# Second projection product moved into the projection's own PSUM bank, with longer mask and sum operations

## The chip, the core and the metric

The kernel runs on one core of a Trainium2 chip. The metric is the device time in microseconds (us) of one execution; the kernel before takes 344.99 us (median of three runs, 344.81 to 345.07). A core has a matrix engine (TensorE, PE in the profile, with its weight loads as PEld), a vector engine (VectorE, DVE), a scalar engine (ScalarE, ACT), GpSimd (POOL) and SyncE (SP). Each works through its own instruction list in order and waits for the others by semaphores.

## The reference

Sliding-window attention with a linear position bias feeds a gated feed-forward layer:

```python
# attention: 8 batches x 8 heads, 576 tokens, head width 64, window 128
scores = scale * q @ k.T + bias;  masked to 0 <= row - col < 128
x = softmax(scores) @ v                     # -> 4608 tokens x 512
# feed-forward: 512 -> 1536 -> 512
g = x @ w_gate;  val = x @ w_val
out = (g * sigmoid(g) * val) @ w_out        # float32
```

The kernel cuts the 4608 tokens into 9 blocks (n = 0 to 8) of 512 tokens, and the hidden width 1536 into 12 slices (m = 0 to 11) of 128. Heavy products run in float16 with float32 sums in PSUM.

## The kernel before

For blocks 0 to 5 each slice m takes two "wide" products of four 128x512 matmuls, `pg` (gate) and `pv` (value). ScalarE takes tanh of half the gate, VectorE makes `uu`, and VectorE multiplies it by `pv` into `hT`:

```python
    def gate(n, m, pg, c0=0, c1=512):
        ...
        nc.scalar.activation(tt, pg[:, c0:c1], AF.Tanh, scale=0.5)
        nc.vector.scalar_tensor_tensor(out=uu, in0=tt, scalar=one if (n, m) == PIN else 1.0,
                                       in1=pg[:, c0:c1], op0=ALU.add, op1=ALU.mult)
    def val(n, m, pv, c0=0, c1=512):
        ...
        nc.vector.tensor_mul(hT[n][:, m, c0:c1], acted[(n, m)][1][:, c0:c1], pv[:, c0:c1])
```

The projection by `w_out` of blocks 1 to 8 is done with seven products in place of eight (Strassen's scheme in Winograd's form). It needs sums of quarters of `hT`, made on VectorE in three parts per block, after slices 9, 10 and 11:

```python
    def four_sums(a11, a12, a21, a22, s2, s3, s4):
        return [lambda: nc.vector.tensor_sub(s3, a11, a21),
                lambda: nc.vector.tensor_add(a21, a21, a22),
                lambda: nc.vector.tensor_sub(s2, a21, a11),
                lambda: nc.vector.tensor_sub(s4, a12, s2)]

    def sums(n, c):
        ...
        lo, hi = slice(2 * c, 2 * c + 2), slice(HM + 2 * c, HM + 2 * c + 2)
        ...
```

One call of `strassen(n, t)` makes two row groups of 128 tokens; there are two calls (t = 0, 1) for a block. Each `product` is six matmuls of 256 columns. X and Y are the two halves of one PSUM tile `po`, which is a whole bank and of which there is one. `half_plus` is a VectorE operation that empties a half of the bank into an output tile and adds an earlier product:

```python
            po = ps_f.tile([P, 2, HC], FP32, name="po", tag="po", bufs=1)
            X, Y = po[:, 0, :], po[:, 1, :]
            p2 = (ps_f.tile([P, HC], FP32, name="p2", tag="gv") if seeded
                  else ps_a.tile([P, HC], FP32, name="p2", tag="a"))
        ...
        product(X, A11, B11, True)                 # P1
        ... nc.scalar.mul(p1s, X, factor)
        yield
        product(p2, A12, B21, not seeded)          # the second product
        ... half_plus(top[:, 0:HC], p2, p1s)
        yield
        product(X, S2, T2);  nc.scalar.mul(u2s, X, factor)
        yield
        product(Y, S1, T1, end);  nc.scalar.mul(p5s, Y, factor)
        yield
        product(X, S3, T3);  half_plus(low[:, HC:DM], X, p5s)
        yield
        product(Y, S4, B22);  half_plus(top[:, HC:DM], Y, u2s)
        store(n, t, top, ...)
        yield
        product(X, A22, T4);  nc.scalar.mul(low[:, 0:HC], X, factor)
        store(n, t + 2, low, ...)
        yield
```

`seeded` holds for blocks 5 to 7 and `end` for block 8. For blocks 1 to 4 neither holds, and the second product takes one of four banks of the pool `ps_a`, tag "a", which attention uses for its scores (`ps`, `psc`), its weighted values (`av`) and its transposes (`px`, `pt`).

The seven products of a call are woven between the 24 wide products of the next block (their index is 2m for the gate and 2m + 1 for the value); the set AT says after which:

```python
    AT = {1, 3, 4, 6, 8, 9, 11, 12, 14, 16, 17, 19, 20, 22}
            ...
            for m in range(NMB):
                for half, _ in enumerate(gate_val(n, m)):
                    yield 1.0
                    if n > 1 and 2 * m + half in AT:
                        next(parts)
                    ... one or two of the waiting sums are issued here
                ...
                if n > 0 and m >= 9:
                    (at_once if n == 1 and m < 11 else later.extend)(sums(n, m - 9))
```

Attention for later blocks is woven in by a counter. A unit of attention has a tile of exponentials `ex` of eight heads by 256: ScalarE makes it in four parts from four banks of scores, VectorE multiplies it by the mask `reg` in two halves:

```python
        def mul(q4):
            if early_tile:
                return
            o = slice(4 * q4, 4 * q4 + 4)
            nc.vector.tensor_mul(e[:, o, :], e[:, o, :], reg[:, o, :])
        return [[products], [lambda: act(0, 0)], [lambda: act(0, 1), lambda: mul(0)],
                [lambda: act(1, 0)], [lambda: act(1, 1), lambda: mul(1)]]
```

From the start of block 2 the order of the PE list is as the program gives it; the lists of VectorE and ScalarE are ordered by the compiler's scheduler.

Of the kernel before, what the change touches and what calls it, by code (L numbers as in the profile page):

```python
# [10 lines left out]
FP32 = mybir.dt.float32  # L11
# [5 lines left out]
P = 128  # L17
# [19 lines left out]
LATE = 13  # L37
# [14 lines left out]
def kernel(  # L52
# [10 lines left out]
    nc = tc.nc  # L63
    B, H, S, D = q.shape
    NTOK, DM = out.shape
# [79 lines left out]
    ps_f = ctx.enter_context(tc.tile_pool(name="ps_f", bufs=3, space=PSUM))  # L145
    ps_a = ctx.enter_context(tc.tile_pool(name="ps_a", bufs=4, space=PSUM))
# [96 lines left out]
    def scores(i):  # L243

        s, p = units[i]
        def combined(n):
            return scores_128(s, (3, 7, 8)[n], 8, (s, "c", n), msk[n])

        def together(one, two):
            return [one[0] + two[0]] + one[1:] + two[1:]  # L250

        if p == 8:
            first = combined(0) if s == 0 else []
            return first + together(combined(1), combined(2))
        if p == 7 and s == 0:
            return scores_128(s, p, p, (s, p), reg[:, :, 0:P])
        if p == 7:
            return together(scores_128(s, p, p, (s, p), reg[:, :, 0:P]), combined(0))
        if p == 3:
            return scores_128(s, p, p, (s, p), reg[:, :, 0:P], i < FIRST)  # L260
        ks = (9 * s + p) % NK
        banks = []
        early_tile = i < FIRST
        e = epool.tile([P, H, 256], FP16, name="ex", tag="ex", bufs=4)
        ex[(s, p)] = e

        def products():
            for q4 in range(2):
                two = [ps_a.tile([P, 2, 256], FP32, name="ps", tag="a") for _ in range(2)]
                banks.append(two)  # L270
                for par in range(2 if early_tile else 0):
                    o = 4 * q4 + 2 * par
                    nc.tensor.matmul(two[par], idm, bias[:, o:o + 2, :], start=True, stop=False)
                for j in range(2):
                    pair = 2 * q4 + j
                    for par in range(2):
                        rows = slice(64 * par, 64 * par + 64)
                        nc.tensor.matmul(two[par][:, j, :], kT[rows, ks, pair, :],  # L278
                                         qT[rows, p:p + 2, pair, :], start=(j == 0 and not early_tile),
                                         stop=(j == 1))  # L280

        def act(q4, par):
            o = 4 * q4 + 2 * par
            nc.scalar.activation(e[:, o:o + 2, :], banks[q4][par], AF.Exp, scale=scale)  # L284

        def mul(q4):
            if early_tile:
                return
            o = slice(4 * q4, 4 * q4 + 4)
            nc.vector.tensor_mul(e[:, o, :], e[:, o, :], reg[:, o, :])  # L290

        return [[products], [lambda: act(0, 0)], [lambda: act(0, 1), lambda: mul(0)],
                [lambda: act(1, 0)], [lambda: act(1, 1), lambda: mul(1)]]

# [196 lines left out]
        for f in fs:  # L491
            f()

    def sums(n, c):

        if n not in hsum:
            hsum[n] = [spool.tile([P, HM, 256], FP16, name=f"S{i}", tag=f"S{i}") for i in (2, 3, 4)]
        lo, hi = slice(2 * c, 2 * c + 2), slice(HM + 2 * c, HM + 2 * c + 2)
        a11, a12 = hT[n][:, lo, 0:256], hT[n][:, hi, 0:256]
        a21, a22 = hT[n][:, lo, 256:512], hT[n][:, hi, 256:512]  # L500
        s2, s3, s4 = (t_[:, lo, :] for t_ in hsum[n])
        return four_sums(a11, a12, a21, a22, s2, s3, s4)

    def strassen(n, t):

        h = hT[n]
        A11, A12 = h[:, 0:HM, 0:256], h[:, HM:NMB, 0:256]
        S1, A22 = h[:, 0:HM, 256:512], h[:, HM:NMB, 256:512]
        S2, S3, S4 = hsum[n]
        cols = slice(t * P, (t + 1) * P)  # L510
        end = n == NBLK - 1
        seeded = SEVEN_FROM <= n + 1 < NBLK
        factor = 1.0 if n >= SEVEN_FROM else 0.5
        if end:
            X, Y = (ps_a.tile([P, HC], FP32, name="po", tag="a", bufs=4) for _ in range(2))
            p2 = ps_f.tile([P, HC], FP32, name="p2", tag="gv")
        else:
            po = ps_f.tile([P, 2, HC], FP32, name="po", tag="po", bufs=1)
            X, Y = po[:, 0, :], po[:, 1, :]
            p2 = (ps_f.tile([P, HC], FP32, name="p2", tag="gv") if seeded  # L520
                  else ps_a.tile([P, HC], FP32, name="p2", tag="a"))
        top, low = (opool.tile([P, DM], FP32, name="osb", tag="osb") for _ in range(2))
        if end and t:
            spare = [opool.tile([P, DM], FP32, name="osb", tag="osb") for _ in range(2)]
            p1s, p5s, u2s = spare[0][:, 0:HC], spare[0][:, HC:DM], spare[1][:, 0:HC]
        else:
            p1s, p5s, u2s = (supool.tile([P, HC], FP32, name=i, tag=i, bufs=1)
                             for i in ("p1s", "p5s", "u2s"))

        def product(dst, a, b, start=False):  # L530
            for m in range(HM):
                nc.tensor.matmul(dst, a[:, m, cols], b[:, m, :], start=(start and m == 0),  # L532
                                 stop=(m == HM - 1), skip_group_check=True)

        def half_plus(dst, a, b):
            nc.vector.scalar_tensor_tensor(out=dst, in0=a, scalar=factor, in1=b,
                                           op0=ALU.mult, op1=ALU.add)

        product(X, A11, B11, True)
        if seeded:  # L540
            nc.scalar.copy(p2, X)
        else:
            nc.scalar.mul(p1s, X, factor)
        yield
        product(p2, A12, B21, not seeded)
        if seeded:
            nc.vector.tensor_scalar_mul(top[:, 0:HC], p2, factor)
        else:
            half_plus(top[:, 0:HC], p2, p1s)
        if end and t:  # L550
            store(n, t, top, 0, HC)
        yield
        product(X, S2, T2)
        nc.scalar.mul(u2s, X, factor)
        yield
        product(Y, S1, T1, end)
        if end and t:
            nc.vector.tensor_scalar_mul(p5s, Y, factor)
        else:
            nc.scalar.mul(p5s, Y, factor)  # L560
        yield
        product(X, S3, T3)
        half_plus(low[:, HC:DM], X, p5s)
        if end and t:
            store(n, t + 2, low, HC, DM, True)
        yield
        product(Y, S4, B22)
        half_plus(top[:, HC:DM], Y, u2s)
        store(n, t, top, HC if end and t else 0, DM, end)
        yield  # L570
        product(X, A22, T4)
        if end:
            nc.vector.tensor_scalar_mul(low[:, 0:HC], X, factor)
        else:
            nc.scalar.mul(low[:, 0:HC], X, factor)
        store(n, t + 2, low, 0, HC if end and t else DM, end)
        yield
# [31 lines left out]
    later = []  # L609
# [86 lines left out]
                    of[which[0]][name](which[1])  # L696
                yield n, 7 * u + k, name, which

    AT = {1, 3, 4, 6, 8, 9, 11, 12, 14, 16, 17, 19, 20, 22}

    def ffn():

        for n in range(NBLK):
# [8 lines left out]
# [5 lines that stand above are left out]
                        yield 0.75  # L717
                    if n > 1:
                        for _ in range(1 + (len(later) > 3)):
                            if later:  # L720
                                later.pop(0)()
                if n == 1:
                    if m in (4, 6, 8, 10):
                        for _ in project(0, m // 2 - 2, ps_f, "po", 1):
                            yield 1.0
                    if m in (4, 6, 8):
                        weight_sums(m // 2 - 2)
                if n > 0 and m >= 9:
                    (at_once if n == 1 and m < 11 else later.extend)(sums(n, m - 9))
                if n + 1 == SEVEN_FROM:  # L730
                    if m == SILU_AT:
                        attention_ends()
                        by_silu.update((n, i) for i in range(m + 1, NMB))
                    if m in (SILU_AT + 1, SILU_AT + 2):
                        later.extend(gate_val_weight_sums(m - SILU_AT - 1))
                    if m == SILU_AT:
                        later.extend(x_sums(n + 1))
# [267 lines left out]
```

## Time and profile before

| what | value |
|---|---|
| time, median of three runs | 344.99 us |
| span of the profiled execution | 343.0 us |
| PE busy | 329.1 us (96%) |
| VectorE busy | 277.5 us (81%) |
| ScalarE busy | 207.6 us (61%) |
| products of the projection for blocks 1 to 4 | from 97 to 248 us of the span |
| granted PE clock, mean of the span | 0.999 |

The page gives the busy time of each engine over the span and in 40 equal slices (a slice is 8.6 us; a digit is the busy share in tenths). Matmuls are pipelined, and the end of each is modelled, so the busy share of the PE is not its share of useful work: starts of neighbouring matmuls must be compared. A line of the timeline gives start, length, engine, line of the program, operation, what is written from what, how many were merged and, in brackets, the idle time before it and what ended it.

### The profile page before, as it was taken

Reading aid. Unit: us, or ns where it says so; the run is one execution under the profiler, and the core shown is the slowest. Engines: PE = TensorE matmul, PEld = TensorE weight load, DVE = VectorE, ACT = ScalarE, POOL = GpSimd, SP = SyncE. Lnnn points to the kernel's source line nnn. Section 1 sums busy time; section 2 is a strip of 40 time slices with the busy share of each in tenths; the row PEclk is TensorE's granted clock in tenths of the full one; section 3 lists DMA queues with packets and bytes.
Section 4 is the critical chain, followed back from the end, with each engine's and each line's share of the span. In section 5 each row is a group of like instructions: output and inputs, shape, how many; then the busy total and the mean of one; then the engine's idle time right before and its main releaser. Section 6 shows DMA issues by size and latency. Waiting matters only on the chain.

```text
span 343.0 us, 7778 instructions
## 1 busy us (share of the span) xinstructions
PE 329.1 (96%) x2983; PEld 218.2 (64%) x2983; DVE 277.5 (81%) x652; ACT 207.6 (61%) x412; POOL 109.6 (32%) x136
## 2 busy tenths in 40 slices
PE   6999989999999999999999999999999999999995
PEld 3484455444456565656565655565788878888884
DVE  6578886999798679988899999999855975775683
ACT  3758676565666755756556547563467666776640
POOL 8968672649674274844017000000000000000000
PEclk9999999999999999999999999999999999999999
DMA  9999999999999999999979912021101101011024
GB/s 153 169 180 176 161 173 149 83 135 163 131 172 140 158 169 169 122 166 136 157 201 135 160 32 78 15 71 39 63 2 61 63 0 64 8 56 63 0 71 116
DMA packets 160037, 37.37 MB, mean 109 GB/s; under 512 B 147328, under 2 KB 155648, under 8 KB 160000
## 3 DMA queue, kind: packets, MB, share of 16 engines
q0 software_dynamic: 118336, 18.62, 84.1%
q1 hardware_dynamic: 40976, 17.64, 28.3%
q10 hardware_dynamic: 688, 0.62, 0.6%
q8 instruction: 23, 0.38, 0.5%
q14 instruction: 14, 0.11, 0.1%
HBM read 37.91 MB, written 9.44 MB: 138 GB/s over the span
## 4 chain that ended last, share of the span: by engine, by line
PE 70%; DVE 19%; ACT 6%; issue 3%; DMA 1%; ACTq 0%; DVEq 0%
PE po L532 15%; PE pg L397 13%; PE pv L397 12%; PE gX L623 8%; PE gY L623 4%; PE av L345 4%; DVE uu L416 3%; DVE hT L427 3%; PE ps L278 3%; PE p L532 2%; PE po L451 2%; PE gZ L623 2%; DVE x L348 2%; ACT ex L284 2%; PE px L371 2%
## 5 line engine op out<-in xcount | busy, mean ns | idle before, releaser
L397 PE MATMUL pv<-xT,wv_sb 128*128 128x512 f16 (+2 forms) x320 | 76.5, 358 | 0.5 <-DVE hT L427 0.2
L397 PE MATMUL pg<-xT,wg_sb 128*128 128x512 f16 (+2 forms) x320 | 75.8, 358 | 0.3 <-DVE xT L373 0.2
L415 ACT ACTIVATE tt<-pg 128x512 f16<-128x512 f32 (+2 forms) x70 | 41.3, 590 | 50.4 <-PE pg L397 49.4
L284 ACT ACTIVATE ex<-ps 128x512 f16<-128x512 f32 x96 | 50.0, 606 | 11.4 <-PE ps L278 11.4
L416 DVE SCALAR_TENSOR_TENSOR uu<-tt,pg 128x512 f16<-128x512 f16 (+2 forms) x69 | 45.8, 664 | 10.5 <-ACT tt L415 10.2
L427 DVE TENSOR_TENSOR hT<-uu,pv 128x512 f16<-128x512 f16 (+2 forms) x70 | 46.5, 665 | 3.6 <-PE pv L397 1.6
L185 POOL DMA_DIRECT2D va<-in_v_dram x40 | 34.2, 862 | 32.8 <-PE av L345 23.9
L397 PEld LDWEIGHTS <-wg_sb 128*128 128x128 f16 x320 | 28.2, 98 | 24.3 <-issue 2.5
L397 PEld LDWEIGHTS <-wv_sb 128*128 128x128 f16 x320 | 28.3, 98 | 24.0 <-issue 2.9
L532 PEld LDWEIGHTS <-hT 128*128 128x128 f16 x384 | 36.8, 98 | 10.4 <-issue 1.1
L191 POOL DMA_DIRECT2D kn<-in_k_dram x39 | 33.3, 858 | 22.0 <-DMA kT<-kn 11.4
L191 POOL DMA_DIRECT2D qn<-in_q_dram x39 | 33.4, 863 | 18.2 <-DMA va<-in_v_dram 11.2
L532 PEld LDWEIGHTS <-S 128*128 128x128 f16 x288 | 27.6, 98 | 10.7 <-issue 2.5
L290 DVE TENSOR_TENSOR ex<-ex,m_reg 128x1024 f16<-128x1024 f16 x42 | 28.6, 685 | 3.2 <-ACT ex L284 3.1
L348 DVE TENSOR_TENSOR x<-av,rec 128x256 f16<-128x256 f32 x72 | 28.5, 418 | 0.4
L532 PE MATMUL po<-T,S 128*128 128x256 f16 x192 | 26.5, 273 | 0.5 <-DVE S L487 0.5
L532 PE MATMUL po<-T,hT 128*128 128x256 f16 x192 | 26.1, 273 | 0.0
L317 ACT ACTIVATE exc<-psc 128x512 f16<-128x512 f32 x40 | 21.3, 608 | 4.1 <-PE psc L313 4.1
L675 DVE TENSOR_TENSOR hT<-s,v 128x512 f16<-128x512 f16 x18 | 7.6, 422 | 18.5 <-ACT s L674 18.5
L345 PEld LDWEIGHTS <-ex 128*128 128x128 f16 x384 | 17.4, 97 | 4.6 <-issue 1.3
L345 PE MATMUL av<-va,ex 128*128 128x65 f16 x384 | 19.3, 193 | 0.7 <-ACT ex L284 0.7
L278 PE MATMUL ps<-qT,kT 64*128 64x256 f16 x192 | 16.6, 272 | 0.4 <-DVE qT L223 0.2
(134 smaller groups left out, 534.9 us busy)
## 6 DMA issues: line engine op xcount, KB each, us to landing
out_dram<-osb SPq DMA_DIRECT2D x32, 256.0 KB, 2.4
va<-in_v_dram POOLq DMA_DIRECT2D x32, 128.0 KB, 8.7
qn<-in_q_dram POOLq DMA_DIRECT2D x31, 128.0 KB, 9.0
kn<-in_k_dram POOLq DMA_DIRECT2D x31, 128.0 KB, 9.5
wg_sb<-in_moe_w_gate_dram POOLq DMA_DIRECT2D x6, 256.0 KB, 7.6
wv_sb<-in_moe_w_val_dram POOLq DMA_DIRECT2D x6, 256.0 KB, 8.2
wo_sb<-in_moe_w_out_dram POOLq DMA_DIRECT2D x2, 768.0 KB, 9.5
kn<-in_k_dram POOLq DMA_DIRECT2D x8, 64.0 KB, 7.3
```

Source lines behind the costliest of these rows:

```text
L185: nc.gpsimd.dma_start(va[rank][p0:p1, :, 0:D], src)
L191: nc.gpsimd.dma_start(t_[p0:p1], src)
L284: nc.scalar.activation(e[:, o:o + 2, :], banks[q4][par], AF.Exp, scale=scale)
L290: nc.vector.tensor_mul(e[:, o, :], e[:, o, :], reg[:, o, :])
L345: nc.tensor.matmul(av[:, j, :], w, val, start=(n == 0), stop=(n == len(todo) - 1))
L348: nc.vector.tensor_mul(x[:, 4 * half:4 * half + 4, :], av[:, :, 0:D], rec.broadcast_to([P, 4, D]))
L397: nc.tensor.matmul(ps[:, c0:c1], w[:, kb, ms], xT[n][:, kb, c0:c1], start=(kb == 0 and c0 == 0), stop=(kb == NKB - 1 and c1 == 512), skip_ ...
L415: nc.scalar.activation(tt, pg[:, c0:c1], AF.Tanh, scale=0.5)
L416: nc.vector.scalar_tensor_tensor(out=uu, in0=tt, scalar=one if (n, m) == PIN else 1.0, in1=pg[:, c0:c1], op0=ALU.add, op1=ALU.mult)
L427: nc.vector.tensor_mul(hT[n][:, m, c0:c1], acted[(n, m)][1][:, c0:c1], pv[:, c0:c1])
L532: nc.tensor.matmul(dst, a[:, m, cols], b[:, m, :], start=(start and m == 0), stop=(m == HM - 1), skip_group_check=True)
L623: nc.tensor.matmul(dst[:, i, :], w[:, kb, c0 + i * P:c0 + (i + 1) * P], a[:, kb, :], start=(start and i == 0 and kb == 0), stop=(i == 1 an ...
```

## The change

For blocks 1 to 4 the seven products are put in a new order and all stay in the bank `po`. The second product A12·B21 comes sixth and is summed in PSUM on top of P1, which ScalarE has copied back from SBUF into Y; so VectorE no longer has to add the two, and no bank of attention's pool is taken. ScalarE then empties Y. The points of weaving (AT) move with it. Two further edits make VectorE operations longer and fewer: from attention unit 13 on, one mask multiplication covers the eight heads, and the sums of a block come in two parts, of four slices and of two. The aim is less work on VectorE.

```diff
         def mul(q4):
-            if early_tile:
+            if early_tile or (q4 == 0 and i >= LATE):          # LATE = 13
                 return
-            o = slice(4 * q4, 4 * q4 + 4)
+            o = slice(0, 8) if i >= LATE else slice(4 * q4, 4 * q4 + 4)
 ...
-    def sums(n, c):
+    def sums(n, c, many=2):
-        lo, hi = slice(2 * c, 2 * c + 2), slice(HM + 2 * c, HM + 2 * c + 2)
+        lo, hi = slice(2 * c, 2 * c + many), slice(HM + 2 * c, HM + 2 * c + many)
 ...
-            p2 = (ps_f.tile([P, HC], FP32, name="p2", tag="gv") if seeded
-                  else ps_a.tile([P, HC], FP32, name="p2", tag="a"))
+            p2 = ps_f.tile([P, HC], FP32, name="p2", tag="gv") if seeded else Y
 ...
+        if not seeded and not end:
+            product(X, A11, B11, True)
+            nc.scalar.copy(p1s, X)
+            yield
+            product(X, S2, T2)
+            nc.scalar.mul(u2s, X, factor)
+            yield
+            product(Y, S1, T1)
+            nc.scalar.mul(p5s, Y, factor)
+            yield
+            product(Y, S4, B22)
+            half_plus(top[:, HC:DM], Y, u2s)
+            nc.scalar.copy(Y, p1s)
+            yield
+            product(X, S3, T3)
+            half_plus(low[:, HC:DM], X, p5s)
+            yield
+            product(Y, A12, B21)
+            nc.scalar.mul(top[:, 0:HC], Y, factor)
+            store(n, t, top)
+            yield
+            product(X, A22, T4)
+            nc.scalar.mul(low[:, 0:HC], X, factor)
+            store(n, t + 2, low)
+            yield
+            return
 ...
-    AT = {1, 3, 4, 6, 8, 9, 11, 12, 14, 16, 17, 19, 20, 22}
+    AT = {1, 4, 5, 7, 8, 10, 11, 13, 15, 16, 18, 19, 21, 22}
 ...
-                if n > 0 and m >= 9:
-                    (at_once if n == 1 and m < 11 else later.extend)(sums(n, m - 9))
+                if n > 0 and m >= 10:
+                    (at_once if n == 1 and m < 11 else later.extend)(sums(n, 2 * m - 20, 24 - 2 * m))
```

## The prediction

> **What bounds the kernel now.** First the page: the busy times, then the slices of the two busiest engines.
>
> ```profile
> PE 329.1 (96%) x2983; PEld 218.2 (64%) x2983; DVE 277.5 (81%) x652; ACT 207.6 (61%) x412; POOL 109.6 (32%) x136
> ...
> PE   6999989999999999999999999999999999999995
> ...
> DVE  6578886999798679988899999999855975775683
> ACT  3758676565666755756556547563467666776640
> ```
>
> The PE is busy nearly throughout, and VectorE reaches nine tenths from the 20th to the 28th slice (163 to 240 us). That stretch lies within blocks 1 to 4 of the seven-product projection, the stage that the change touches. Busy time by stretches (length, PE, PEld, DVE, ACT, then POOL, clock, DMA) sharpens this:
>
> ```profile
> 160.00:180.00 20.00, 19.38 (x197) 12.04 (x196) 18.67 (x45) 11.67 (x24) 2.99 (x4) 1.00 1.51 171
> 180.00:200.00 20.00, 19.16 (x170) 11.41 (x168) 18.99 (x47) 11.12 (x23) 6.35 (x9) 1.00 1.43 128
> 200.00:220.00 20.00, 19.34 (x168) 11.18 (x167) 19.85 (x50) 12.02 (x25) 0.00 (x0) 1.00 0.20 53
> 220.00:240.00 20.00, 20.00 (x180) 12.50 (x179) 19.84 (x52) 10.26 (x20) 0.00 (x0) 1.00 0.17 47
> ```
>
> VectorE has 2.7 us to spare in 80, ScalarE 35. Both the PE and VectorE are close to full, so the question is how much PE time VectorE really costs. The list of PE waits between 97 and 248 us answers it:
>
> ```profile
> PE po L532 <- DVE osb L536: 1.5, 2, 0.8
> PE p L532 <- ACT ex L284: 0.7, 1, 0.7
> PE po L532 <- DVE S L487: 0.5, 1, 0.5
> PE psc L313 <- DVE osb L536: 0.2, 1, 0.2
> ```
>
> These are 2.9 us of modelled idle time. Ends of matmuls are modelled, so I also compared starts: a wide product takes four times 0.216 us, a projection product six times 0.109. Measured so, the same waits are 0.78 and 1.11 us (po behind osb), 0.96 (p), 0.68 (S) and 0.35 (psc), together 3.9 us. **This is about all that relief of VectorE and of attention's banks can give back**; other lost PE time in this stage is some 0.4 us at each group of score matmuls, which the change leaves.
>
> The chain of waits shows one such wait, and the pace of the PE after it:
>
> ```profile
> 188.23 0.35 DVE osb L536
> 188.57 0.04 issue
> 188.62 0.81 PE po L532 x6
> 189.43 0.86 PE pg L397 x4
> 190.29 0.86 PE pv L397 x4
> 191.16 0.48 PE av L345 x16
> 191.64 0.66 PE po L532 x6
> ```
>
> The product at 188.62 is S4·B22, which writes Y. The operation before it, in full in the timeline, is the `half_plus` that reads **X**:
>
> ```profile
> 188.15 0.42 DVE L536 SCALAR_TENSOR_TENSOR osb<-po,p5s 128x256 f32<-128x256 f32 x1
> ...
> 188.62 0.81 PE L532 MATMUL po<-wo_sb,S 128*128 128x256 f16 x6 [0.84 <-DVE osb L536]
> ```
>
> So a write to one half of the bank waits for the reader of the other half. This decides the case.
>
> [...] The trace agrees: the wait above, and 0.05 to 0.06 us from the end of the X reader to the start of the Y product in four of eight such places (110, 129, 168, 188 us). [...]
>
> ```profile
> 206.08 0.42 DVE L486 TENSOR_TENSOR hT<-hT 128x512 f16<-128x512 f16 x1
> 206.41 0.68 DVE L416 SCALAR_TENSOR_TENSOR uu<-tt,pg 128x512 f16<-128x512 f16 x1
> 207.01 0.42 DVE L487 TENSOR_TENSOR S<-hT 128x512 f16<-128x512 f16 x1
> 207.34 0.42 DVE L536 SCALAR_TENSOR_TENSOR osb<-po,u2s 128x256 f32<-128x256 f32 x1
> 207.68 0.68 DVE L290 TENSOR_TENSOR ex<-ex,m_reg 128x1024 f16<-128x1024 f16 x1
> 208.28 0.68 DVE L427 TENSOR_TENSOR hT<-uu,pv 128x512 f16<-128x512 f16 x1
> ```
>
> From start to start, 512 elements in float16 take 0.33 us, 1024 take 0.60: joining saves 2 x 0.33 - 0.60, about 0.07 us, and not the 0.15 that the overlapping lengths (0.42, 0.68) suggest. [...] here lengths average 0.358 us against 0.216 from start to start, hence the use of starts.
>
> **The change, part by part.** Counts are from the instruction lists of the two compiled kernels.
>
> Saved on VectorE: 8 `half_plus` (two calls in each of four blocks) x 0.34 = 2.7 us; 15 joined masks x 0.07 = 1.0 us; 20 joined sums (three parts to two, four operations, five blocks) x 0.07 = 1.4 us. Together 5.1 us, some 4.7 of them between 97 and 248 us: 3%. Added on ScalarE: 16 operations of 128x256 (copy back to Y, emptying of A12·B21) x 0.38 us (the row of `u2s`) = 6.1 us, on an engine that is 39% idle. PE work is unchanged.
>
> Off the PE's path: the wait for a bank of attention (0.96), the two waits of S4 behind `half_plus` (1.89; S4 now comes two wide products after S1, and the product after the other `half_plus` also has two between), the psc wait behind the removed addition (0.35) and perhaps the wait for sums (0.68; the sums are shorter but start one slice later, so I count half). Sum: 3.5 us.
>
> Onto the PE's path: S3·T3 follows S4·B22 with one wide product between. It writes X of the same bank, so it waits until `half_plus` has read Y **and** ScalarE has copied P1 into Y. From the first S4 matmul: six matmuls 0.65, drain of the last 0.165 (0.273 less 0.109), hand-over 0.04, `half_plus` 0.415, hand-over 0.04, copy 0.37, hand-over 0.04: 1.72 us at least. With one wide product between, S3 would be due at 0.65 + 0.86 = 1.52 us. So even empty queues cost 0.2 us. Queues are not empty: in the kernel before, the `half_plus` after S4 ends 0.89 us after it on average, against 0.46 at the quickest.
>
> The order of ScalarE's list adds more. Of the eight copies, three (in the first calls of blocks 2, 3 and 4) stand **behind the tanh of the gate product that lies between S4 and S3**. There S3 waits for that product (due at 1.52), its drain 0.165, hand-over 0.04, tanh to next start 0.49, copy 0.37, hand-over 0.04: 2.62 us, 1.1 late, three times 3.3 us. In the second call of block 1 four exponentials (4 x 0.48 us, started with scores just ahead of S4) delay the copy: about 0.8 us. The second calls of blocks 3 and 4 have a bare value product between: 0.2 plus the usual 0.4 of queue, 0.6 each, 1.2. The other two (first call of block 1, second of block 2) have 0.48 us of attention between as well: 0.2 each, 0.4. Sum: 5.7 us.
>
> Shorter distances elsewhere (S2 to S1, A12 to A22: one wide product and one ScalarE operation, 1.27 us needed of 1.52) should cost 0.4 us in all, where ScalarE is late.
>
> Net: -3.5 + 5.7 + 0.4 = +2.6 us. Some of it falls where VectorE is behind anyway and catches up while the PE waits; I take 1 us off for that: **346.6 us**.
>
> **Rivals.** First, VectorE is the true limit from 160 to 240 us. For it: 97% busy. Against it: only 2.9 of the 3.9 us of waits lie there, and the PE is full from 220 to 240. If it holds, new waits of the PE hide behind VectorE's work, and the 2.6 us of VectorE work saved there come out: 342 to 343.5 us. Second, the single bank becomes a serial chain from PE to VectorE to ScalarE to PE, and the delays spread to exponentials and tanh: 349 to 350 us. For it: the copies waiting at the head of ScalarE's list for `half_plus`. Against it: ScalarE has room. Third, nothing shows, because gains and waits cancel: 344.5 to 345.5 us.
>
> **Range and chances.** The mean of my sum is slightly slower; the eight S3 waits are the largest term and could be 2.5 or 8 us. I predict 346.6 us, range 343.0 to 349.6. A gain of over 2% (below 338.1) would need 7 us, more than all the waits there are: 0.02. A loss of over 2% (above 351.9) needs every copy to be late by more than a microsecond: 0.05. Within 2%: 0.93.
>
> **What would show it.** In the list of PE waits, S3·T3 behind ScalarE's copy into po, eight times with 5 to 6 us in all, the three longest about 1 us; no wait of p, and no S4 behind `half_plus`. VectorE busy about 8 us less in summed lengths (5 in true occupancy), ScalarE 6 more. Wrong would be: no wait at S3 (then the halves are not one object, or the queues are quick), or VectorE still full with the PE no later.

## The result and the profile after

The changed kernel takes **353.69 us** (median of four runs, 352.9 to 354.54) against 344.90 us: a ratio of 1.0255, 95% interval 1.0222 to 1.0289. It is slower by 8.8 us; predicted were 1.7 us, and a range that ended at 349.6. The four times lie in two pairs: 352.90 us twice, and 354.47 and 354.54 us. In the second pair the mean granted PE clock was 0.993, against 0.999 and 0.998 in the first, which the last section takes up; the profile below is of the run of 354.54 us.

The page of the changed kernel, in the lines that answer to those of before:

```profile
PE 332.4 (94%) x2983; PEld 220.0 (62%) x2983; DVE 274.4 (78%) x609; ACT 212.7 (60%) x428; POOL 109.6 (31%) x136
...
PE   7999989999999999799897989979999999999995
DVE  6568877999887779767997889987665785785583
```

The slices are now 8.8 us each. VectorE has less to do and ScalarE more, as meant (609 operations for 652, 428 for 412). But the PE, solid nines before in the stretch of blocks 1 to 4, now has sevens and eights, and VectorE's nines there have thinned out: both became less full. Nothing new is at its limit; something now makes the engines wait for each other. The first matmul of the stage begins at 97.1 us (97.3 before) and what follows its last takes 98.5 us (98.6 before). The stage itself grew from 147.2 to 157.2 us. All of the loss is there. In it VectorE is now idle for 24.5 us, where it was idle for 11.6 before: its work is not what limits the changed kernel.

The PE's waits between 97 and 248 us (total, times, longest):

```profile
PE po L531 <- ACT po L550: 9.4, 7, 2.1
PE po L531 <- ACT osb L556: 0.5, 1, 0.5
```

L550 is the copy of P1 into Y, and the product that waits for it is S3·T3, which writes X. The waits of before (p behind attention, S4 behind `half_plus`, S2 behind the sums) are gone, as predicted; this one took their place. VectorE's wait for exponentials ahead of the mask, the second in its list before, is now its longest; before and then after:

```profile
DVE ex L290 <- ACT ex L284: 2.3, 6, 0.8
```

```profile
DVE ex L290 <- ACT ex L284: 9.0, 9, 2.0
```

One of the longest waits, in the timeline of the changed kernel (first call of block 3):

```profile
187.06 1.23 DVE L290 TENSOR_TENSOR ex<-ex,m_reg 128x2048 f16<-128x2048 f16 x1 [0.87 <-ACT ex L284]
...
187.30 0.82 PE L531 MATMUL po<-wo_sb,S 128*128 128x256 f16 x6
...
187.95 1.03 PE L397 MATMUL pg<-xT,wg_sb 128*128 128x512 f16 x4
188.20 0.68 DVE L416 SCALAR_TENSOR_TENSOR uu<-tt,pg 128x512 f16<-128x512 f16 x1
...
188.92 0.69 DVE L427 TENSOR_TENSOR hT<-uu,pv 128x512 f16<-128x512 f16 x1
...
189.52 0.41 DVE L348 TENSOR_TENSOR x<-av,rec 128x256 f16<-128x256 f32 x1
...
189.94 0.39 DVE L535 SCALAR_TENSOR_TENSOR osb<-po,u2s 128x256 f32<-128x256 f32 x1
...
190.43 0.38 ACT L550 COPY po<-p1s 128x256 f32<-128x256 f32 x1 [0.81 <-DVE osb L535]
...
190.85 0.81 PE L531 MATMUL po<-T,S 128*128 128x256 f16 x6 [1.87 <-ACT po L550]
```

Read it from below. S3 waits 1.87 us for the copy; the copy waits 0.81 us for `half_plus` (L535), with ScalarE idle; and `half_plus` starts 1.8 us after S4 ended (187.30 + 0.82), because five operations and the tail of the mask stand ahead of it in VectorE's list. VectorE had stood idle for 0.87 us just before that mask. Two suspects stem from this: the chain through one bank (S4, `half_plus`, copy, S3), and the joined mask that must wait for four exponentials. How late S3 starts is best seen from the starts: it comes 3.55 us after S4 (190.85 less 187.30), and without a wait it would come 1.52 us after it, so it is 2.03 us late.

To compare runs I use one figure besides the time: the PE time lost at the projection products of the stage, that is, how much later each of their matmuls starts than the pace of the matmul before it allows. It is 4.6 us before and 12.7 after. It is good to about 0.3 us, since the matmuls of scores start in close pairs and have no single pace (in the kernel before 2 to 4 ns between the two of a pair, and from a pair to the next mostly 0.05 us for `psc` and 0.11 for `ps`).

### The profile page after: what moved, and what is told of

Its sections match the earlier page's. It is cut to its first block, busy times and chain, and to the rows that moved or that the text cites. A ratio compares the mean times of both kernels' runs of the same rounds, so it can differ in the third digit from the quotient of the medians.

```text
span 352.8 us, 7747 instructions
## 1 busy us (share of the span) xinstructions
PE 332.4 (94%) x2983; PEld 220.0 (62%) x2983; DVE 274.4 (78%) x609; ACT 212.7 (60%) x428; POOL 109.6 (31%) x136
## 4 chain that ended last, share of the span: by engine, by line
PE 71%; DVE 15%; ACT 9%; issue 3%; DMA 1%; ACTq 0%; DVEq 0%
PE po L531 16%; PE pv L397 13%; PE pg L397 13%; PE gX L649 8%; PE gY L649 4%; ACT ex L284 3%; PE av L345 3%; PE po L451 3%; PE ps L278 3%; DVE uu L416 3%; PE gZ L649 2%; DVE ex L290 2%; DVE hT L427 2%; PE px L371 2%; DVE x L348 1%
## 5 line engine op out<-in xcount | busy, mean ns | idle before, releaser
L397 PE MATMUL pv<-xT,wv_sb 128*128 128x512 f16 (+2 forms) x320 | 77.4, 361 | 0.6 <-DVE uu L416 0.3
L290 DVE TENSOR_TENSOR ex<-ex,m_reg 128x2048 f16<-128x2048 f16 (+1 forms) x27 | 26.5, 984 | 9.8 <-ACT ex L284 9.7
L531 PE MATMUL po<-wo_sb,hT 128*128 128x256 f16 x144 | 19.7, 273 | 0.0
```

The costliest lines, as they stand in the source:

```text
L397: nc.tensor.matmul(ps[:, c0:c1], w[:, kb, ms], xT[n][:, kb, c0:c1], start=(kb == 0 and c0 == 0), stop=(kb == NKB - 1 and c1 == 512), skip_ ...
```

## The experiments

Each was timed against the kernel before on the same chip. In the table "lost" is the figure just defined.

| kernel | time, us | ratio to before, 95% interval | lost, us |
|---|---|---|---|
| before | 344.9 to 345.2 | 1 | 4.6 |
| changed | 353.69 | 1.0222 to 1.0289 | 12.7 |
| changed, masks in halves | 351.88 | 1.0182 to 1.0216 | 11.5 |
| changed, sums in three parts | 354.82 | 1.0253 to 1.0294 | 12.6 |
| changed, masks and sums as before | 352.52 | 1.0206 to 1.024 | 11.7 |
| changed, copy after S3 | 349.22 | 1.0105 to 1.0135 | 8.0 |
| changed, two wide products between S4 and S3 | 347.40 | 1.0046 to 1.0076 | 6.9 |
| changed, ScalarE empties Y | 345.50 | 0.9998 to 1.0018 | 4.7 |
| the same, masks in halves | 345.36 | 0.9999 to 1.0015 | 4.8 |
| the same, and two wide products | 344.31 | 0.9973 to 0.9986 | 4.1 |
| the same, and ScalarE empties X after S3 | 342.89 | 0.9924 to 0.9949 | 2.2 |
| before, joined masks alone | 346.60 | 1.0025 to 1.0054 | 5.6 |
| before, joined sums alone | 344.12 | 0.9958 to 0.9981 | 3.6 |
| before, joined sums, ScalarE empties X after S3 | 343.39 | 0.9938 to 0.9963 | 2.7 |

The rows' times differ from that of before as their lost times do, to within 1 us in all but one: this is where most of the 8.8 us are. The exception (1.8 us, with the sums in three parts) is mostly the clock: its mean was 0.994 to 0.995 in three of the four runs of that kernel, but 0.998 in the profiled one, which took 353.38 us.

**Masks in halves again.** In the changed kernel:

```diff
-            if early_tile or (q4 == 0 and i >= LATE):
+            if early_tile:
...
-            o = slice(0, 8) if i >= LATE else slice(4 * q4, 4 * q4 + 4)
+            o = slice(4 * q4, 4 * q4 + 4)
```

> The changed kernel with the mask multiplication in two halves again. Theory 1 (the joined mask multiplication waits in VectorE's in-order list for all four exponentials and so holds up the half_plus behind S4, on which the copy and S3 wait): waits of S3 behind the copy fall from 10.9 us to about 6, VectorE's waits for exponentials before the mask from 9 us to 2 or 3; about 348.5 us. Theory 2 (the chain PE - half_plus - copy - PE through the one bank costs this by itself, whatever the masks are): 352 to 354 us, waits at S3 still near 10 us.

Measured: 351.88 us. VectorE's wait for exponentials fell from 9.0 to 4.4 us, but `half_plus` still ends 1.53 us after S4 on average over the eight calls (1.58 with the joined mask), and only 1.2 us of lost time came back. The PE's wait at S3 is nearly as long as with the joined mask (9.4):

```profile
PE po L531 <- ACT po L550: 8.4, 7, 1.8
```

The joined mask, my first suspect, is a minor part: with half of its idle time gone, other work still stands ahead of `half_plus`.

**Sums in three parts again.**

```diff
-                if n > 0 and m >= 10:
-                    (at_once if n == 1 and m < 11 else later.extend)(sums(n, 2 * m - 20, 24 - 2 * m))
+                if n > 0 and m >= 9:
+                    (at_once if n == 1 and m < 11 else later.extend)(sums(n, m - 9))
```

> The changed kernel with the sums of hT in three parts again, from slice 9 on. Theories 1 and 2 both expect no effect beyond 1 us: 352.7 to 354.5 us, waits at S3 near 10 us. Theory 3 (the later, longer sums delay VectorE at the end of each block, and with it half_plus): 350 us or less.

Measured: 354.82 us, 0.3 above the range of theories 1 and 2; the one run in which the clock did not fall took 353.38. The lost time is the same (12.6 and 12.7). The joined sums are not to blame.

**The new order alone**: both of these edits at once.

> The changed kernel with both masks and sums as before: only the new order of products, with the copy back into Y. Theory 1: as with the masks alone put back, 348 to 349 us. Theory 2: 352 to 354 us. If the new order were a gain by itself, under 345 us.

Measured: 352.52 us, against 344.9 to 345.2 before. So the new order of products with its copy, and nothing else, costs 7.4 us. That is theory 2, without regard to the mask.

**The copy after S3.**

```diff
             half_plus(top[:, HC:DM], Y, u2s)
-            nc.scalar.copy(Y, p1s)
             yield
             product(X, S3, T3)
             half_plus(low[:, HC:DM], X, p5s)
+            nc.scalar.copy(Y, p1s)
             yield
```

> The changed kernel with ScalarE's copy of P1 into Y issued after S3 and its half_plus, two wide products before A12 B21 needs it: S3 now waits for half_plus of Y alone. Theory 2 (the copy in S3's path is the cost): nearly all comes back, 344 to 346.5 us. Theory 1 (half_plus itself comes 1.6 us after S4 on average, as it stands behind the joined mask): S3 still waits about 1 us each for half_plus, 8 us less 0.45 us each, so 349 to 350 us.

Measured: 349.22 us, the half: 4.5 us came back. The PE's waits between 97 and 248 us now begin with

```profile
PE po L531 <- DVE osb L535: 6.0, 5, 1.6
```

S3 writes X and waits for `half_plus` that reads Y: again the reader of one half holds up a write to the other. (Both halves lie in the one tile `po`, so no run here tells a guard of the tile from one of the bank.) The copy's own share is 4.7 us of lost time (12.7 less 8.0), about 0.6 for each of the eight; the rest is a late `half_plus`. My theory 2 had put too much on the copy, theory 1 had the right size here for a reason that the first run had already refuted.

**Two wide products between S4 and S3** (S4 earlier, then A12·B21 earlier too):

```diff
-    AT = {1, 4, 5, 7, 8, 10, 11, 13, 15, 16, 18, 19, 21, 22}
+    AT = {1, 4, 5, 6, 8, 9, 11, 13, 15, 16, 17, 19, 20, 22}
```

> The changed kernel with S4 one place earlier in AT (6 for 7, 17 for 18) and A12 B21 one earlier (9 for 10, 20 for 21): two wide products between S4 and S3, one between S3 and A12 B21. Theory 2 (the distance is too short for the chain half_plus - copy): waits at S3 fall by about 0.86 us each, from 10.9 to 4 or 5 us, at A12 at most 2 us; 347 to 349 us. Theory 5 (VectorE is late anyway and the waits only move): 352 us or more, the waits at A12 grow as those at S3 shrink.

Measured: 347.40 us. Waits at S3 fell to 2.4 us of modelled idle time, and 1.4 us appeared behind the other `half_plus`, before A12·B21. Distance helps as theory 2 says; theory 5, under which the waits would only have moved, is out.

**ScalarE empties Y**, so that VectorE's list is no longer in the chain. The copy into Y still is:

```diff
-            half_plus(top[:, HC:DM], Y, u2s)
+            nc.scalar.copy(top[:, HC:DM], Y)
+            half_plus(top[:, HC:DM], top[:, HC:DM], u2s)
             nc.scalar.copy(Y, p1s)
```

> The changed kernel with ScalarE emptying Y after S4 (a copy into the output tile), half_plus adding in SBUF afterwards, off the chain: 8 more ScalarE operations of 128x256, as many on VectorE. The chain from S4 to S3 no longer passes VectorE's list. Theory 6 (half_plus is late because it stands behind 2 us of other work in VectorE's list): waits at S3 fall from 10.9 to 3 to 5 us; 346.5 to 348.5 us. Theory 2 without the list (any two hand-overs are too long): waits near 8 us, 351 us.

Measured: 345.50 us, better than expected: with one edit, and one ScalarE operation more per call, 8.2 us came back (7.4 against the two runs in which the clock did not fall). The PE's wait at S3, 9.4 us in the changed kernel, is

```profile
PE po L531 <- ACT po L551: 1.0, 1, 1.0
```

In the timeline of this kernel, the same place as above:

```profile
184.28 0.82 PE L531 MATMUL po<-wo_sb,S 128*128 128x256 f16 x6
...
185.14 0.37 ACT L549 COPY osb<-po 128x256 f32<-128x256 f32 x1 [0.64 <-PE po L531]
...
185.54 0.38 ACT L551 COPY po<-p1s 128x256 f32<-128x256 f32 x1
...
185.97 0.81 PE L531 MATMUL po<-T,S 128*128 128x256 f16 x6
```

S4 ends at 185.10, ScalarE is there 0.04 us later, and the two copies and S3 follow without a gap of more than 0.05 us. S3 is 0.17 us late by starts (1.69 us after the start of S4 against 1.52 due), in seven of the eight calls between nothing and 0.18 us, and 1.19 us in one, where exponentials stand ahead of the copies in ScalarE's list. `half_plus` itself comes no earlier than in the changed kernel: it ends 1.75 us after S4 on average (1.58 there), but no product waits for it. The chain through ScalarE is thus nearly harmless as such; **what cost most of the 8.8 us was that a link of it stood in VectorE's busy list.** No run moved `half_plus` forward within that list, so why the scheduler puts it so late stays open.

**Masks in halves on top of this:**

> The changed kernel with ScalarE emptying Y after S4 and the mask in halves again. Theory 1 (the joined mask costs VectorE idle time, here too): 344 to 345 us against 345.5 with the joined mask. Theory 4 (joined masks cost only where a half_plus on the tight chain stands behind): no difference, 345.2 to 345.8 us.

Measured: 345.36 us, no difference (theory 4): here no product waits for what stands behind the mask, and joining costs nothing.

**Joined masks or joined sums alone, in the kernel before:**

```diff
-            if early_tile:
+            if early_tile or (q4 == 0 and i >= LATE):
...
-            o = slice(4 * q4, 4 * q4 + 4)
+            o = slice(0, 8) if i >= LATE else slice(4 * q4, 4 * q4 + 4)
```

> The kernel before with only the joined mask multiplication. Putting the halves back in the changed kernel gave 1.8 us. Theory 1 (joining costs by itself, since VectorE stands idle until all four exponentials are there): 346 to 347 us, VectorE's waits for exponentials about 9 us against 2.3. Theory 4 (the wait matters only where a half_plus on the tight chain stands behind it): within 1 us of the kernel before, 344 to 346 us, though VectorE waits as long.

> The kernel before with only the sums in two parts. In the changed kernel, putting the three parts back cost about 1 us, within noise. All theories: 343.8 to 345.2 us, S2 behind the sums no worse than the 0.7 us of before; over 346 us would mean that the later start of the sums costs.

Measured: masks 346.60, 1.4 us slower; sums 344.12, 1.1 us faster. The masks' time lies in the range of theory 1, but the PE's waits fit theory 4: S4 behind `half_plus` grew from 1.5 to 2.2 us of modelled idle time, since the kernel before has such a link too, from S3 to S4 (`half_plus` of X ends 1.38 us after S3 on average, 1.18 before). VectorE waited 4.3 us for exponentials, not the expected 9. For the sums the wait of S2 (0.5 us) is gone and S4 waits 1.1 us instead of 1.5; on average `half_plus` of X is no quicker (1.16 us after S3).

**Towards a better kernel.** From the run with ScalarE emptying Y and masks in halves: first the AT with two wide products, then also `half_plus` of X after S3 replaced in the same way (a ScalarE copy into `low`, the addition afterwards in SBUF).

> As the run before, and S4 and A12 B21 one place earlier in AT, so that two wide products lie between S4 and S3. The remaining waits at S3 (0.17 us each and one of 1.2) go, but half_plus of X before A12 B21 is now one wide product ahead of it and may be waited for, 1.5 to 2.5 us as in the run with two wides. If that wait is as long: 344.5 to 346 us, no gain; if the emptier VectorE list is quick there: 343 us.

> As the run before, and ScalarE empties X after S3 as well, so that no product of blocks 1 to 4 waits for VectorE: all waits of po behind VectorE and the copy under 1.5 us together apart from the sums. 342.5 to 343.8 us, faster than both kernels. If ScalarE is overfull instead (16 operations more than before the run above): waits for tanh and exponentials grow and 345 us or more results.

Measured: 344.31 us, just under the range named for no gain, and **342.89 us**. In the last one the PE waits for only one thing from 97 to 248 us:

```profile
PE po L531 <- DVE S L487: 0.9, 1, 0.9
```

The same cure in the kernel before, with the joined sums:

```diff
-        half_plus(low[:, HC:DM], X, p5s)
+        if seeded or end:
+            half_plus(low[:, HC:DM], X, p5s)
+        else:
+            nc.scalar.copy(low[:, HC:DM], X)
+            half_plus(low[:, HC:DM], low[:, HC:DM], p5s)
```

> The kernel before with the sums in two parts and, in blocks 1 to 4, ScalarE emptying X after S3 so that S4 no longer waits for half_plus in VectorE's list (0.6 and 0.5 us of modelled idle time, about 1.6 by starts, with the sums joined). If the list is the cause there too: 342.3 to 343.3 us. If ScalarE is no quicker there: 344 us as with the sums alone.

Measured: 343.39 us, between its two forecasts and nearer to the first; 1.7 of the 2.2 us by which the last kernel beats the kernel before need no new order of products. The joined sums alone had brought 1.1 of them.

## Why the prediction was wrong

- **The bound and what could be won back: right.** The waits of p, S4 and S2 went, about the 3.9 us that starts had shown (3.7 with the pace of the matmul before taken off everywhere). The work moved as forecast: VectorE's summed lengths fell by 8.1 us, ScalarE's rose by 6.3. One slip in reading changes nothing: VectorE's eight full slices are the 21st to the 28th, from 171 us on.
- **The new wait: right place, wrong size.** I named S3 behind the copy, eight times, with 5.7 us in all. By starts it is 10.9 us: 0.42, 0.92, 2.03, 1.14, 2.04, 1.79, 2.24 and 0.28. The first, second and last of these were put at 1.6 us together and took 1.6, the delay by four exponentials (0.8 put, 0.92 measured) among them. The other five were put at 4.1 us and took 9.2: the whole miss is there. I gave a loss of over 2% a chance of 0.05 because it would need every copy to be over a microsecond late; five of eight were enough.
- **The step that failed is "queues are not empty".** I took the delay of `half_plus` after S4 from the kernel before: 0.89 us on average, 0.43 over the quickest. In the changed kernel it is 1.58 us, and in these five 1.8 to 2.4. The same operation had moved to another place in the list: in the call shown above it now stands behind a mask, a `uu`, an `hT` and parts of two normalisations. In the kernel before, the `half_plus` of X, which already stood ahead of a product one wide product away, ended 1.18 us after S3; that row was nearer, though still too low.
- **The tanh ahead of the copy was the wrong reason for the long waits.** In the three calls where I charged 1.1 us for it, 2.03, 2.04 and 2.24 us were lost, but ScalarE had passed the tanh and stood idle (0.81 us above) until `half_plus` was done. One of the calls that I called nearly free (0.2) lost 1.14 and one that I put at 0.6 lost 1.79, for the same cause.
- **The 1 us taken off was wrong.** I let VectorE catch up while the PE waits. But in the changed kernel it is idle too (24.5 us of the stage, 11.6 before), so nothing was caught up; that its next work comes from the waiting PE is my reading. The second rival (a serial chain of PE, VectorE, ScalarE and PE) is what happened, beyond its own figure of 349 to 350 us.
- **Smaller terms:** the shorter distances were put at 0.4 us; the wait behind the emptying of A12·B21 has 0.5 us of modelled idle time. Lost time rose from 4.6 to 12.7, by 8.1 us; the two runs in which the clock did not fall are 8.0 us slower than before. The rest of the 8.8 is the clock, below.

## What to carry to other kernels

When a change puts a bank's reader between two products, count not its length (0.39 us for `half_plus` here) but its place in the in-order list of its engine (it ended up to 2.4 us after the product): what is released just before it, and what that waits for. A short operation that the matrix engine waits for belongs on the engine that is idle when it is needed, even if it takes an operation more; here a ScalarE copy of 0.37 us in place of a VectorE addition of 0.39 us that came 1.8 us late was worth 7.4 us. Joining operations saves little (0.07 us each) and can make the joined one wait for its last input: the joined masks alone cost 1.4 us, the joined sums alone won 1.1. Do it where nothing urgent stands behind.

## What the runs showed of the hardware that I had not expected

After the longest wait of the changed kernel (2.08 us of idle PE, until 231.14) the granted clock fell: the trace has it at half from 231.52 us for 3.41 us, and at full in the rest of the stage. The stretch from 231 to 236 us (length, PE, PEld, DVE, ACT, POOL, clock, DMA share, GB/s):

```profile
231.00:236.00 5.00, 4.86 (x39) 2.58 (x39) 4.27 (x10) 2.21 (x6) 0.00 (x0) 0.66 0.13 27
```

At 233.2 us the matmuls of a wide product started 0.40 to 0.43 us apart instead of 0.216, and the product took 1.67 us from its start to that of the next, 0.8 more than at full clock. Four waits of 1.0 to 1.9 us lay in the 82 us before that of 2.1 us. Only this profile shows the place, but the mean clocks and times of the runs suggest how often it happened and what it cost:

| kernel | runs with a mean clock of 0.995 or less: clock, us | the other runs: clock, us |
|---|---|---|
| changed | 2: 0.993, 354.47 and 354.54 | 2: 0.998 and 0.999, 352.90 |
| changed, sums in three parts | 3: 0.994 to 0.995, 354.71 to 354.95 | 1: 0.998, 353.38 |
| changed, masks and sums as before | 1: 0.992, 353.65 | 3: 0.997 to 1.0, 352.30 to 352.60 |

All runs of the other kernels have 0.997 or more. The runs with the lower clock are 1.2 to 1.6 us longer than the others of their kernel, and they occur only in kernels with long waits at S3 (8.6 to 9.4 us of modelled idle time in the three profiles; with masks in halves 8.4, and there no run has it). Waits of 1.9 us in the same run, and one of 2.0 us in the profile of the last kernel of this table, did not bring it on, so what sets it off stays open.
